# Token numbers of expert tiles: by 0/1 matrix products on TensorE instead of a table of places in DRAM

## Chip, cores, metric

One core of a Trainium2 chip. The time is the device time of one execution in microseconds (us). "Profiled span" is the time from the first to the last instruction in the one execution that was profiled; it is some 2 us shorter than the time of the same execution. Runs are compared with runs of the kernel before on the same chip, fast runs with fast runs; a run is called slow here when it takes over 1.5% more than the fastest one of its kernel.

## The reference, cut

```python
# attention: 8 batches x 8 heads, 576 positions, head size 64, window 32, dilation 4 in half the heads
scores = np.where(masks, scale * q @ k.T, -1e9)
x = softmax(scores) @ v                            # -> (8, 576, 512): 4608 tokens
# experts: 8, each 512 -> 1024 -> 512
for b in range(B):
    prev_e = -1
    for s in range(S):
        fresh_e = int(np.argmax(logits[b, s]))     # logits = x @ w_gate
        if s == 0 or local_gate[b, s] < 0.5:       # local_gate = sigmoid(x @ w_local)
            e = fresh_e
        else:
            e = prev_e if prev_e >= 0 else fresh_e
        prev_e = e
        out[b, s] = p[e] * (np.maximum(x[b, s] @ w1[e], 0.0) @ w2[e])
```

## The kernel before

TensorE first does the attention, two heads at a time (32 "pairs"), and then the experts, in 40 tiles of 128 tokens that have one expert. Every eight pairs complete a "group" of 1152 tokens, which is routed: its tokens' experts are found, and their ranks among the tokens of the same expert. After two groups the first 11 tiles are full and can begin while the attention still runs ("level 0"); the others follow after the fourth group ("level 1"). To begin, a tile needs the list of its tokens, one per partition: token number, gate, and two row numbers in the attention's output.

Before, this list comes from a table in DRAM. Each token is written as a row of four floats (16 bytes) at its place, 128 tokens by one indirect write, nine writes per group; each level then reads its tiles' rows back and transposes them.

```python
def place(g):                                     # (cut) kp = rank of each token within its expert
    nc.vector.tensor_tensor(pl, kp, cst[:TB, C_BASE:C_CODE].unsqueeze(2).to_broadcast(shape), op=Alu.add)
    nc.vector.tensor_tensor(pl, pl, st["oh"], op=Alu.mult)
    nc.vector.tensor_reduce(pf, pl.rearrange("p e j -> p j e"), axis=AX.X, op=Alu.add)
    nc.vector.tensor_copy(pi, pf)
    st["places"] = pi

def scatter(g, j):                                # 9 per group, 36 in all
    i = nc.gpsimd.indirect_dma_start(
        out=tab, out_offset=bass.IndirectOffsetOnAxis(ap=routes[g]["places"][:, j:j + 1], axis=0),
        in_=pay[:, g, j], in_offset=None)

def rows(lv):                                     # one read per level, after all writes so far
    i = nc.gpsimd.indirect_dma_start(out=tr..., in_=tab..., in_offset=...ri...)

def tokens(lv, c):                                # four per level
    tp = bank([P, nt], "tt")
    nc.tensor.transpose(tp, tr[:, :, (2, 3, 0, 1)[c]], ident[:nt, :nt])
    nc.vector.tensor_copy(tiles[what, lv], tp)
```

The order on TensorE is fixed when the program is built. The loop over the pairs counts nominal time ("gaps"); at a gap the next waiting step of the routing is put into TensorE's stream, if its nominal time has passed.

```python
def gap(us):
    gaps[0] += us
    if waiting and gaps[0] - last[0] >= waiting[0][0]:
        last[0] = gaps[0]
        waiting.pop(0)[1]()

def values(n):                                    # (cut) the second product of a pair
    for (a, z), pr in zip(UNITS, prob.pop(n)):
        ...                                       # 20 or 16 products into pv, then VectorE scales
        if not a:
            gap(1.0)                              # a step may stand here, after 20 of the 36

def overlap(n):                                   # the pair's 32 overlapping rows
    nc.vector.tensor_copy(vt[:WIN, :, 1:], vt[QB:, :, :NB - 1])

def idle(times):                                  # products of zeros; also in the kernel before
    to = bank([P, 4, P], "idle")
    for i in range(times):
        nc.tensor.matmul(to, lhsT=blank, rhs=blank.unsqueeze(1).to_broadcast([P, 4, P]), start=True, stop=True, ...)
```

## Time and profile before

| | before |
|---|---|
| median of 3 runs | 788.26 us |
| profiled span | 783.0 us |
| last product on TensorE begins | 770.12 us |
| from there to the end ("tail") | 12.9 us |
| first tile's feature transposes | 160.9 us |
| TensorE clock halved, before the tail | 37.5 us |
| DMAs issued by GpSimd | 241 |

The halved clock is a sum of the trace's clock records (6.8 us from 83.7, 23.9 from 128.1, 6.8 from 281.7). The lines of the slices and of TensorE's timeline are in the prediction.

### The profile page before, as it was taken

How to read it: one execution, taken by the hardware profiler on the slowest of the kernel's cores; microseconds unless marked ns; L12 is line 12 of the kernel's file. 1: busy time of each engine (PE TensorE's matmuls, PEld its weight loads, DVE VectorE, ACT ScalarE, POOL GpSimd, SP SyncE). 2: the span in 40 equal slices, each digit the busy share in tenths (PEclk: the TensorE clock that was granted, in tenths of full speed). 3: DMA queues.
4: the chain of work that ended last, by engine and by line, in shares of the span. 5: the costliest groups of instructions: out<-in, count | busy, mean ns of one | idle time of the engine just before them, and what ended most of it. 6: DMA issues, size and time to landing. Idle time of an engine off the chain costs nothing. (4 is left out here: it accounts for less than half of the span.)

```text
span 783.0 us, 15857 instructions
## 1 busy us (share of the span) xinstructions
PE 745.7 (95%) x6012; PEld 558.9 (71%) x6012; DVE 187.6 (24%) x492; ACT 119.6 (15%) x213; POOL 232.1 (30%) x245
## 2 busy tenths in 40 slices
PE   8999897989999979999999999999999999999993
PEld 5877676977766748678677668677677687687781
DVE  5868494534214110110111010111011011101100
ACT  2545343221120000000001000001001000000000
POOL 1003123232723544312332332332332332333100
PEclk9999897699999989999999999999999999999997
DMA  9868869970584872492167113840113830621000
GB/s 319 302 233 245 232 192 268 410 298 28 120 283 147 183 286 78 149 316 64 35 225 256 35 35 98 306 134 33 34 48 109 306 108 28 194 101 31 25 26 19
DMA packets 37032, 124.06 MB, mean 158 GB/s; under 512 B 7955, under 2 KB 8083, under 8 KB 36944
## 3 DMA queue, kind: packets, MB, share of 16 engines
q1 hardware_dynamic: 27152, 101.92, 39.0%
q0 software_dynamic: 9792, 20.99, 9.7%
q8 instruction: 52, 0.85, 0.5%
q14 instruction: 36, 0.29, 0.1%
HBM read 207.90 MB, written 20.88 MB: 292 GB/s over the span
## 5 line engine op out<-in xcount | busy, mean ns | idle before, releaser
L685 PEld LDWEIGHTS hp<-xe,w1s 128*128 128x128 f32 x2560 | 292.4, 192 | 20.7 <-issue 17.4
L685 PE MATMUL hp<-xe,w1s 128*128 128x128 f32 x2560 | 295.0, 275 | 2.6 <-DVE bad L811 1.5
L700 PE MATMUL yp<-w2s,h 128*128 128x512 f32 x640 | 284.7, 597 | 0.0
L700 PEld LDWEIGHTS yp<-w2s,h 128*128 128x128 f32 x640 | 118.8, 191 | 132.9 <-issue 132.7
L656 POOL DMA_INDIRECT xg<-xd,plain x80 | 76.8, 960 | 263.3 <-PE yp L700 235.5
L689 ACT ACTIVATE h<-hp 128x512 f32<-128x512 f32 x80 | 47.8, 597 | 530.0 <-PE hp L685 530.0
L656 POOL DMA_INDIRECT xg<-xd,dilated x80 | 75.7, 946 | 64.0 <-PE yp L700 55.2
L707 DVE TENSOR_SCALAR y<-yp,gate 128x512 f32<-128x512 f32 x40 | 30.0, 750 | 238.5 <-PE yp L700 130.0
L675 DVE COPY xe<-tp 128x512 f32<-128x512 f32 x40 | 27.6, 691 | 245.1 <-PE tp L673 245.1
L518 POOL DMA_INDIRECT tab<-cst,pi x36 | 35.5, 987 | 115.2 <-DVE x L353 63.5
L294 PE MATMUL sc<-kq 64*96 64x64 f32 x1152 | 62.8, 262 | 6.2 <-DMA kq<-in_qk_dram 5.3
L294 PEld LDWEIGHTS sc<-kq 64*96 64x96 f32 x1152 | 57.3, 175 | 14.7 <-issue 10.3
L708 POOL DMA_INDIRECT out_dram<-y,tok x40 | 40.2, 1006 | 76.5 <-DVE y L707 59.5
L301 DVE SCALAR_TENSOR_TENSOR pr<-sc,mk 96x640 f32<-96x640 f32 x64 | 47.8, 751 | 50.0 <-PE sc L294 33.7
L304 ACT ACTIVATE pr<-pr 96x640 f32<-96x640 f32 x64 | 43.4, 683 | 90.8 <-DVE pr L301 86.9
L347 PE MATMUL pv<-vt,pr 96*64 96x65 f32 x1152 | 45.6, 236 | 4.5 <-issue 4.5
L347 PEld LDWEIGHTS pv<-vt,pr 96*64 96x64 f32 x1152 | 40.2, 148 | 7.3 <-issue 4.8
L370 PE MATMUL tp<-cst,x 128*128 128x128 f32 x144 | 24.5, 309 | 4.0 <-DVE x L353 2.3
L353 DVE TENSOR_TENSOR x<-pv,rec 128x320 f32<-128x320 f32 x64 | 26.8, 449 | 0.1
L673 PE MATMUL tp<-cst,xg 128*128 128x128 f32 x160 | 24.2, 273 | 0.0
L240 DVE COPY vt<-vt 32x1040 f32<-32x1040 f32 x32 | 22.6, 706 | 3.7 <-DMA vt<-in_v_dram 2.8
L370 PEld LDWEIGHTS tp<-cst,x 128*128 128x128 f32 x144 | 17.8, 156 | 7.9 <-PE tp L370 3.2
(109 smaller groups left out, 158.3 us busy)
## 6 DMA issues: line engine op xcount, KB each, us to landing
w1s<-in_w_dram SPq DMA_DIRECT2D x160, 512.0 KB
w2s<-in_w_dram SPq DMA_DIRECT2D x160, 512.0 KB
kq<-in_qk_dram SPq DMA_DIRECT2D x32, 592.0 KB
vt<-in_v_dram SPq DMA_DIRECT2D x32, 292.5 KB
xd<-x SPq DMA_DIRECT2D x16, 576.0 KB
xg<-xd,plain POOLq DMA_INDIRECT x80, 3.0
xg<-xd,dilated POOLq DMA_INDIRECT x80, 3.2
out_dram<-y,tok POOLq DMA_INDIRECT x40, 4.3
```

The source lines that it names most:

```text
L294: here[:] = [nc.tensor.matmul(sc[:KW, u, (i - a) * QB:(i - a + 1) * QB], lhsT=kt[h, i * QB:i * QB + KW], rhs=qt[h, i * QB:(i + 1) * QB], s ...
L301: nc.vector.scalar_tensor_tensor(pr[:, :, :w], sc[:KW, :, :w], -CEIL, mk[:, at:at + w].unsqueeze(1).to_broadcast([KW, 2, w]), Alu.max, Alu ...
L304: nc.scalar.activation(pr[:, :, :w], pr[:, :, :w], Act.Exp, scale=SCALE)
L347: here[:] = [nc.tensor.matmul(pv[u * QB:(u + 1) * QB, i - a], lhsT=pr[:, u, (i - a) * QB:(i - a + 1) * QB], rhs=vt[:, u, i], start=True, s ...
L370: nc.tensor.transpose(tp[:, i].rearrange("p u q -> p (u q)"), x[:, c * w + i].rearrange("p g d -> p (g d)"), ident)
L518: i = nc.gpsimd.indirect_dma_start(out=tab, out_offset=bass.IndirectOffsetOnAxis(ap=routes[g]["places"][:, j:j + 1], axis=0), in_=pay[:, g ...
L656: i = nc.gpsimd.indirect_dma_start(out=xg[t][:, kk], out_offset=None, in_=xd if full == ROWS else xd[:full], in_offset=bass.IndirectOffset ...
L685: here[:] = [nc.tensor.matmul(hp[:, m], lhsT=w1s[t % 2][:, half * FK // 2 + m, kk], rhs=x[:, kk], start=(kk == 0), stop=(kk == DK - 1))]
L689: nc.scalar.activation(ht[t][:, half * FK // 2:(half + 1) * FK // 2], hp, Act.Relu)
L700: here[:] = [nc.tensor.matmul(yp, lhsT=h[:, m], rhs=w2s[t % 2][:, m], start=(m == 0), stop=(m == FK - 1))]
L707: nc.vector.tensor_scalar(y, yp, of_tile("gate", t), None, Alu.mult)
L708: nc.gpsimd.indirect_dma_start(out=out, out_offset=bass.IndirectOffsetOnAxis(ap=of_tile("tok", t), axis=0), in_=y, in_offset=None, bounds_ ...
```

## The change

The intent: no small transfers beside the attention, and no trip through DRAM before the first tile. A token's tile and its place in the tile are known from its rank (`seek`). For each group, `mark` makes two 0/1 matrices on VectorE, "token has place p" and "token is in tile t" (the latter times the four numbers), and `put` multiplies them on TensorE: the sum over tokens is the list.

```diff
-    def scatter(g, j): ...          # 36 indirect writes of places
-    def rows(lv): ...               # 2 reads of the table
-    def tokens(lv, c): ...          # 8 transposes
-    fill ...                        # first contents of the table, 2 DMAs
+    def seek(lv):                   # (cut) tile and place of each token so far
+        q, bound = of_tokens(tiles["off", lv], "q"), of_tokens(tiles["bound", lv], "of_bound")
+        ... q = rank + off, zero where the token is not in this level; hi = q >> 7; at = q - 128 * hi
+    def mark(lv, g):
+        by_place = xp.tile([TB, NJ, P], F32, name="by_place", tag="x")
+        nc.vector.tensor_tensor(by_place, cst[:TB, C_NUM:C_PAY]..., tiles["place"][:, g]..., op=Alu.is_equal)
+        nc.vector.tensor_tensor(there, cst[:TB, C_NUM:C_NUM + nt]..., tiles["tile"][:, g]..., op=Alu.is_equal)
+        by_tile = xp.tile([TB, NJ, TW, nt], F32, name="by_tile", tag="x")
+        for w in range(TW):
+            nc.vector.tensor_tensor(by_tile[:, :, w], there, pay[:, g, :, w]..., op=Alu.mult)
+    def put(lv, g):
+        tp = bank([P, TW, nt], "put")
+        for j in range(NJ):
+            nc.tensor.matmul(tp, lhsT=by_place[:, j], rhs=by_tile[:, j], start=(j == 0), stop=(j == NJ - 1))
+        if not g:
+            tiles["there", lv] = once.tile([P, TW, nt], F32, name=f"there{lv}")
+            nc.vector.tensor_copy(tiles["there", lv], tp)
+        else:
+            nc.vector.tensor_tensor(tiles["there", lv], tiles["there", lv], tp, op=Alu.add)
+        ...
     def route(g):
-        waiting.extend((1.2 if j else 1.5, lambda j=j: scatter(g, j)) for j in range(NJ))
         if lv is not None:
-            waiting.append((0.0, lambda: rows(lv)))
-            waiting.extend((0.0 if c else 12.0 if g == NG - 1 else 9.0, lambda c=c: tokens(lv, c)) for c in range(4))
+            steps.append((1.0, lambda g: seek(lv)))
+            for h in range(g + 1):
+                waiting.append((2.5, lambda h=h: mark(lv, h)))
+                waiting.append((3.5, lambda h=h: put(lv, h)))
```

## The prediction

> **What bounds the kernel now.** I read the page's busy shares first, then the slices, then TensorE's instructions in order of time, then the stretches of 4 us around each hole. The chain that ended last is no help: it holds only the final store.

> ```profile
> PE 745.7 (95%) x6012; PEld 558.9 (71%) x6012; DVE 187.6 (24%) x492; ACT 119.6 (15%) x213; POOL 232.1 (30%) x245
> PE   8999897989999979999999999999999999999993
> DVE  5868494534214110110111010111011011101100
> PEclk9999897699999989999999999999999999999997
> ```

> TensorE is the bound: busy 95% of 783 us, and after about 160 us without a break. VectorE is second, but only in the first 160 us, where the 32 pairs of heads go. The clock line falls in three places (slices 5, 7 to 8, and 15), and a hole in TensorE's stream precedes each. TensorE's timeline has them:

> ```profile
> 80.27 1.75 PE L294 MATMUL sc<-kq 64*96 64x64 f32 x36
> 81.94 0.34 PE L347 MATMUL pv<-vt,pr 96*64 96x65 f32 x4
> 85.70 2.00 PE L347 MATMUL pv<-vt,pr 96*64 96x65 f32 x32 [3.42 <-issue]
> 87.63 2.18 PE L370 MATMUL tp<-cst,x 128*128 128x128 f32 x9
> ...
> 122.32 1.27 PE L347 MATMUL pv<-vt,pr 96*64 96x65 f32 x36
> 128.69 3.15 PE L294 MATMUL sc<-kq 64*96 64x64 f32 x36 [5.10 <-DMA kq<-in_qk_dram]
> ...
> 160.85 0.66 PE L673 MATMUL tp<-cst,xg 128*128 128x128 f32 x4
> ...
> 277.34 1.88 PE L700 MATMUL yp<-w2s,h 128*128 128x512 f32 x4
> 283.21 0.30 PE L610 MATMUL tt<-cst,tr 32*128 32x32 f32 x1 [3.98 <-DMA tr<-tab,ri]
> 283.43 3.78 PE L700 MATMUL yp<-w2s,h 128*128 128x512 f32 x4
> ```

> Holes of 3.42, 5.10 and 3.98 us, and after each the same work takes longer: 36 score products 3.15 instead of 1.75 us, 4 of L700 3.78 instead of 1.88. The first two come while the 9 writes of 128 places each (L518) of a routed group are in the queues; the third is the reading back of the table (L597) itself, at the second level. The first expert tile starts at 160.85, in pair 30. The stretches around the second hole:

> ```profile
> 116.00:120.00 4.00, 3.31 (x68) 2.80 (x66) 3.91 (x11) 1.75 (x3) 3.09 (x4) 1.00 0.63 251
> 120.00:124.00 4.00, 3.42 (x75) 3.05 (x75) 2.75 (x9) 2.30 (x6) 2.90 (x4) 1.00 1.21 219
> 124.00:128.00 4.00, 0.00 (x0) 0.00 (x0) 0.92 (x4) 0.59 (x1) 0.22 (x1) 1.00 0.91 195
> 132.00:136.00 4.00, 4.00 (x45) 3.58 (x43) 1.90 (x6) 1.90 (x4) 0.92 (x1) 0.50 1.01 397
> 136.00:140.00 4.00, 4.00 (x53) 3.81 (x54) 1.51 (x2) 1.24 (x3) 0.00 (x0) 0.50 1.04 421
> ```

> The last three columns are clock, DMA share, GB/s. With the place writes in flight the DMA engines are full (1.21) at 219 GB/s; ten microseconds later they are as full at 397 to 421. The clock stays at 0.50 until about 151.5.

> [...] the L518 writes take 8.5 us (median) to land, 12.1 at most, for 2 KB each. [...] 0.50 from 1.6 us into the hole of 3.42 us and at the end of the one of 5.10, and no drop at waits of 1.07 or 1.46 us. [...] The first hole cuts a run of equal products in two after the fourth, with no semaphore named, so a delayed fetch on full DMA engines is my reading; the trace shows the instruction queue's 52 packets, not the wait. [...]

> **The change, part by part.**

> Removed: 36 writes of places, 2 table reads, the fill of the table, 8 small transposes (0.1 to 0.2 us each), about 8 short VectorE operations per level. GpSimd's time for them (35.5 us) is off every path.
> - Hole 1: 3.42 us, and the slowed work behind it (pv 2.00 for 1.13, turn 2.18 for 1.34, logits 4.60 for 4.22): 2.1. Gain 5.5 us.
> - Hole 2: 5.10 us, and half a clock from 128 to 151.5: 11.7. Gain 16.8 us, provided that nothing else stops TensorE there (see rivals).
> - Hole 3: 3.98 us and 2.8 of slow L700 (3.78 and 2.50 for two times 1.76). Gain 6.8, and 0.6 from the transposes.
> Sum 29.7 us.

> Added on TensorE: a `put` is 9 fp32 products of 128 x 128 stationary by 44 columns (level 0: 4 x 11 tiles) or 128 (level 1: 4 x 32). A program product is two instructions (640 L700 are 40 tiles x 8 products x 2), so 18 each. L685 has the shape of level 1: 64 in 7.31 us, 0.114 each, so 2.06 us per put. I take the same for 44 columns, since loading 128 stationary columns seems to set the pace (4 feature transposes start 0.44 us ahead of what follows, 0.11 each). Level 0 has 2 puts, 4.1 us; level 1 has 4, 8.2 us. All of it is on the bounding engine. Sum 12.3 us.

> Added on VectorE: [...] Level 0: [...] some 6 us, in pairs 21 to 25. A pair lasts 3.68 us there (pairs 4 and 5, 24.27 to 31.63) and costs VectorE 2 x 0.751 + 2 x 0.449 + 2 x 0.166 + 0.706 = 3.44. So it has 0.24 us to spare per pair, and 6 us over five pairs lengthen them by some 5. TensorE's 4.1 us fall into the same pairs, so not both count: I add 2 us to the puts. At level 1 VectorE is a tenth busy and hides its 18 us; but the first put follows seek and mark closely (the emission leaves some 6 us for 6.5), so 1 us of waiting.

> Moved: counting the nominal gaps that the loop hands out, I get the first tile at pair 30 for the kernel before (the trace agrees) and at pair 27 after: the table read's 9 units of wait and the places' 10 go, two marks and puts come. This by itself makes no TensorE work disappear. Its worth is that pairs 28 to 31 lie beside expert work, so the loads of pairs (0.88 MB each) and the first two tiles' weights (8 MB) no longer pace TensorE. As a check by time: pair 18 at 88.8 instead of 94.27, pair 22 at 107.0 instead of 112.47, five pairs with marks and puts 24.8, so pair 27 at 131.8 and the first tile at 133.5; three more pairs remain than before, 11.0 us. 144.5 against 160.85: 16.3 won up to there (5.5 + 16.8 - 6). Level 1 then costs 8.2 + 1.0 - 6.8 - 0.6 = 1.8.

> The two ways agree: 29.7 - 12.3 - 2 - 1 = 14.4, and 16.3 - 1.8 = 14.5. Sum: 788.26 - 14.5 = 773.8; I say **773.5 us**, 1.9% faster.

> **Rivals.**
> - The weights keep the DMA engines full in pairs 21 to 27 with or without places, and TensorE stops there anyway. For it: 1.02 busy from 132 to 168, and 2.2 MB per pair want 5.4 us at 405 GB/s against 3.7 of a pair. Against it: loads go out three pairs ahead, some 11 us, and 1.7 us per pair over six pairs do not use that up; by then the tile has joined. It would give back 5 to 8 us: 779 to 782.
> - VectorE becomes the bound in pairs 22 to 25. The marks take their buffers from the same four as the attention's rows, which are free only when a store to DRAM has landed; [...] VectorE may stop behind it. TensorE would idle long enough to lose its clock again. 778 to 783.
> - The puts cost less: with 44 columns at half the pace, and inside holes that VectorE makes anyway, level 0 is all but free, and short waits of 0.3 to 0.9 us in the pairs vanish under expert work. 767 to 770.
> - Nothing gained: the holes are instruction fetches that come whatever is written. Only hole 3 is then saved and 12 us are added: 790. Against it: a saturated DMA at 397 to 421 GB/s from 132 to 152 stops nothing.

> **Range and chances.** The centre lies almost on the 2% line (772.5). Misses by new waits in pairs 22 to 27 (each a hole plus lost clock, 5 to 9 us) are about as likely as puts and marks that cost 3 to 6 us less than counted. The range is 765 to 783. Faster by over 2%: 0.45; within 2%: 0.52; slower by over 2%: 0.03, as 30 us of holes would all have to stay and the puts cost double.

> **What would show it.** TensorE's busy time 745.7 + 12 less some 8 to 15 us for records made at half clock; clock line at 9 in slices 5 to 8 and 15; no TensorE wait over 2 us between 60 and 160 us and none at level 1; puts as 36 + 72 instructions of 128 x 44 and 128 x 128, 0.11 us apart; first feature transpose near 133 us; marks' comparison 1.2 to 1.4 us; VectorE 9 tenths or more in pairs 22 to 25. I am wrong if a hole over 3 us stands in pairs 22 to 27, if the clock still reads 0.5 there, or if TensorE waits at the puts of level 1.

VectorE's times for `seek` and `mark` (6 us at level 0, 18 at level 1, 6.5 ahead of the first put there) are estimates; no trace of the kernel before has these operations.

## More of the kernel before

One view that I did not read before predicting is the end of the span. These are its stretches of 5 us; the columns are busy time and instructions of PE (TensorE), PEld (its weight loads), DVE (VectorE), ACT (ScalarE) and POOL (GpSimd), then TensorE's clock, DMA share and GB/s:

```profile
770.00:775.00 5.00, 0.71 (x2) 0.00 (x0) 0.75 (x1) 0.00 (x0) 0.97 (x1) 0.82 0.18 61
775.00:780.00 5.00, 0.00 (x0) 0.00 (x0) 0.00 (x0) 0.00 (x0) 0.00 (x0) 0.50 0.02 5
780.00:785.00 5.00, 0.00 (x0) 0.00 (x0) 0.00 (x0) 0.00 (x0) 0.00 (x0) 0.50 0.00 0
```

From about 775 us no engine counts as busy, yet the span ends only at 783.0.

## The result

| | before | after |
|---|---|---|
| median of the 4 runs of this comparison | 788.53 us (787.34 to 790.63) | 793.88 us (793.36 to 795.14) |
| profiled span | 783.0 | 792.3 |
| last product on TensorE begins | 770.12 | 770.64 |
| tail | 12.9 | 21.6 |
| first tile's feature transposes | 160.9 | 148.3 |
| clock halved before the tail | 37.5 | 30.7 |
| DMAs issued by GpSimd | 241 | 201 |

The ratio of fast runs is 1.0067 (95% interval 1.0042 to 1.0092). It divides the mean time of one kernel's fast runs by that of the other's of the same rounds, so it is not quite the ratio of the medians quoted. The change lost 5 us where 14.5 were predicted to be won.

The page of the kernel after, busy shares and two lines of its 40 slices (19.8 us each; a digit is tenths busy, or tenths of the full clock):

```profile
PE 754.4 (95%) x6112; PEld 570.3 (72%) x6112; DVE 205.7 (26%) x535; ACT 119.4 (15%) x213; POOL 194.7 (25%) x205
PE   8999979899999999999999999999999999999990
PEclk9999985899999999999999999999999999999995
```

The clock's falls in slices 5 and 15 are gone, but slices 6 to 8 still show 8, 5, 8. The last PE digit has gone from 3 to 0: TensorE has no work in the last 20 us. TensorE's timeline of the kernel after (start, duration, engine, line, product; in brackets the wait before it; L337 here is L347 before, L284 is L294, L678 is L673):

```profile
111.37 0.80 PE L337 MATMUL pv<-vt,pr 96*64 96x65 f32 x20
116.83 4.07 PE L605 MATMUL put<-by_tile,by_place 128*128 128x44 f32 x18 [4.65 <-DVE by_tile L595]
120.83 1.14 PE L337 MATMUL pv<-vt,pr 96*64 96x65 f32 x16
...
124.00 3.15 PE L284 MATMUL sc<-kq 64*96 64x64 f32 x36
...
140.76 1.75 PE L284 MATMUL sc<-kq 64*96 64x64 f32 x36
...
148.30 0.42 PE L678 MATMUL tp<-cst,xg 128*128 128x128 f32 x2
```

One hole, 4.65 us, before the first `put`, which stands after 20 of the 36 value products of pair 22. From then to about 141 us everything takes almost twice its time: 36 score products 3.15 us instead of 1.75, each `put` 4.07 (2.18 at full clock in e9). VectorE's timeline in the hole shows what TensorE waits for:

```profile
113.63 0.17 DVE L580 TENSOR_SCALAR tile<-tile 128x18 f32<-128x18 f32 x1
113.72 1.35 DVE L587 TENSOR_TENSOR by_place<-cst,at 128x1152 f32<-128x1152 f32 x1
114.99 0.25 DVE L591 TENSOR_TENSOR there<-cst,tile 128x99 f32<-128x99 f32 x1
115.27 0.69 DVE L235 COPY vt<-vt 32x1040 f32<-32x1040 f32 x1
116.00 0.78 DVE L595 TENSOR_TENSOR by_tile<-there,cst 128x99 f32<-128x99 f32 x4
```

The last of `seek` ends at 113.8, and the marks follow with hardly a break, a copy for the next pair (L235) between them. No buffer and no DMA holds VectorE up there: it is simply late. The stretches of 4 us say the same; their columns are as above:

```profile
104.00:108.00 4.00, 3.74 (x74) 3.27 (x75) 3.86 (x23) 1.80 (x4) 0.00 (x0) 1.00 0.72 223
108.00:112.00 4.00, 4.00 (x106) 3.80 (x102) 4.00 (x16) 1.37 (x2) 0.00 (x0) 1.00 0.65 170
112.00:116.00 4.00, 0.17 (x6) 0.03 (x2) 3.94 (x12) 1.30 (x2) 0.00 (x0) 0.69 0.92 351
116.00:120.00 4.00, 3.17 (x15) 3.17 (x16) 2.20 (x8) 0.00 (x0) 0.00 (x0) 0.50 1.01 396
```

From 104 to 116 VectorE (third pair of numbers) is busy 11.80 of 12 us, while TensorE comes down to 0.17 of 4 in the third stretch and the clock with it. And the end of the span of the kernel after:

```profile
770.00:775.00 5.00, 1.23 (x3) 0.19 (x1) 0.75 (x1) 0.00 (x0) 0.97 (x1) 1.00 0.16 57
775.00:780.00 5.00, 0.00 (x0) 0.00 (x0) 0.00 (x0) 0.00 (x0) 0.00 (x0) 0.57 0.03 7
780.00:785.00 5.00, 0.00 (x0) 0.00 (x0) 0.00 (x0) 0.00 (x0) 0.00 (x0) 0.50 0.00 2
785.00:790.00 5.00, 0.00 (x0) 0.00 (x0) 0.00 (x0) 0.00 (x0) 0.00 (x0) 0.50 0.00 0
```

The work ends as before, within half a microsecond; the empty tail is 8.7 us longer. In the tail the trace has instructions that do not count as busy. On GpSimd three long ones stand at the end, two that the trace names INC_SWDGE_SEM and a DRAIN; what comes between and after them is short (0.31 us at most each). Their times from the trace's records, in ns:

```
kernel    GpSimd DMAs   first   second   DRAIN
before    241            732      701     2273
after     201           2082     2070     7832
```

They take 12.0 instead of 3.7 us together, 8.3 us more: nearly the whole difference in the tails.

### The profile page after: what moved, and what is told of

Its sections match the earlier page's. It is cut to its first block, busy times and chain, and to the rows that moved or that the text cites.

```text
span 792.3 us, 15999 instructions
## 1 busy us (share of the span) xinstructions
PE 754.4 (95%) x6112; PEld 570.3 (72%) x6112; DVE 205.7 (26%) x535; ACT 119.4 (15%) x213; POOL 194.7 (25%) x205
## 5 line engine op out<-in xcount | busy, mean ns | idle before, releaser
L284 PEld LDWEIGHTS sc<-kq 64*96 64x96 f32 x1152 | 54.6, 168 | 7.6 <-issue 5.5
L284 PE MATMUL sc<-kq 64*96 64x64 f32 x1152 | 59.8, 256 | 0.2 <-DVE pr L291 0.2
L294 ACT ACTIVATE pr<-pr 96x640 f32<-96x640 f32 x64 | 43.5, 684 | 78.4 <-DVE pr L291 74.2
L337 PE MATMUL pv<-vt,pr 96*64 96x65 f32 x1152 | 44.4, 232 | 0.3 <-issue 0.2
L337 PEld LDWEIGHTS pv<-vt,pr 96*64 96x64 f32 x1152 | 39.0, 144 | 3.5 <-issue 0.6
L360 PE MATMUL tp<-cst,x 128*128 128x128 f32 x144 | 23.5, 299 | 4.2 <-DVE x L343 3.0
L678 PE MATMUL tp<-cst,xg 128*128 128x128 f32 x160 | 24.8, 276 | 1.1 <-DMA xg<-xd,dilated 1.1
L363 ACT COPY xt<-tp 128x384 f32<-128x384 f32 x48 | 21.1, 503 | 25.7 <-PE tp L360 25.1
L235 DVE COPY vt<-vt 32x1040 f32<-32x1040 f32 x32 | 22.3, 697 | 5.2 <-DMA vt<-in_v_dram 4.2
```

The source lines that it names most:

```text
L284: here[:] = [nc.tensor.matmul(sc[:KW, u, (i - a) * QB:(i - a + 1) * QB], lhsT=kt[h, i * QB:i * QB + KW], rhs=qt[h, i * QB:(i + 1) * QB], s ...
L294: nc.scalar.activation(pr[:, :, :w], pr[:, :, :w], Act.Exp, scale=SCALE)
L337: here[:] = [nc.tensor.matmul(pv[u * QB:(u + 1) * QB, i - a], lhsT=pr[:, u, (i - a) * QB:(i - a + 1) * QB], rhs=vt[:, u, i], start=True, s ...
L360: nc.tensor.transpose(tp[:, i].rearrange("p u q -> p (u q)"), x[:, c * w + i].rearrange("p g d -> p (g d)"), ident)
```

## Theories

A: three things ate the gain: (1) the hole before the first `put`, for want of VectorE time; (2) the half clock that follows, because the pairs' small products do not bring the clock back; (3) GpSimd's longer end. B, the rival on the time: the place writes were not what cost time before, the holes come whatever is written. C, the rival on the tail: it belongs to what the last tiles do, not to the number of DMAs.

## The experiments

All results are correct. Every edit is to the kernel after, except where it says otherwise. "Before" is the median of the kernel before on the same chip. "End of work" is the start of the last product; work, tail and half clock are of the profiled run.

| run | median (runs) | before | ratio, 95% | end of work | tail | half clock | first tile | GpSimd DMAs |
|---|---|---|---|---|---|---|---|---|
| e1 | 784.71 | 787.71 | 0.9945 (0.9878 to 1.0011) | 762.86 | 21.2 | 20.5 | 145.0 | 201 |
| e2 | 782.91 | 787.71 | 0.9935 (0.9879 to 0.9991) | 761.75 | 21.2 | 10.2 | 141.6 | 201 |
| e3 | 783.28 | 787.71 | 0.9966 (0.9902 to 1.003) | 764.72 | 13.1 | 13.7 | 142.1 | 237 |
| e4 | 779.53 (3) | 787.71 | 0.9919 (0.9824 to 1.0013) | 764.58 | 13.2 | 13.7 | 141.7 | 237 |
| e5 | 787.89 (1, state unknown) | 786.1 | none | 772.82 | 13.2 | 44.4 | 163.1 | 241 |
| e6 | 794.56 | 786.1 | 1.0112 (1.0041 to 1.0182) | 771.31 | 21.1 | 30.7 | 147.4 | 201 |
| e7 | 786.4 | 786.1 | 1.0 (0.9926 to 1.0075) | 759.82 | 23.8 | 0.0 | 139.6 | 219 |
| e8 | 782.4 (1, state unknown) | 786.1 | none | 767.19 | 13.4 | 13.7 | 147.5 | 237 |
| e9 | 773.02 (6) | 784.28 | 0.9877 (0.9837 to 0.9917) | 758.09 | 13.0 | 0.0 | 137.9 | 237 |
| e10 | 785.11 | 784.28 | 0.9989 (0.9944 to 1.0034) | 768.16 | 21.5 | 30.7 | 143.2 | 201 |
| e11 | 789.12 | 784.28 | 1.0053 (1.0021 to 1.0085) | 766.01 | 21.3 | 10.2 | 144.3 | 201 |
| e12 | 770.17 (5) | 784.28 | 0.9817 (0.979 to 0.9844) | 755.67 | 12.9 | 0.0 | 135.4 | 237 |

The half clock of the table is that of one execution. The mean granted clock of every execution is on record, and within one kernel the time goes with it: e10 took 781.44 and 781.58 us at 0.981 and 0.982, 788.64 and 791.5 (the profiled one) at 0.971; e3 took 779.56 at 0.985 and 787.46 at 0.974. In a span of 780 us, 0.010 of mean clock are some 16 us at half clock (an estimate). So the length of the half clock can change from one execution of a kernel to the next. It is steady in the kernel after (0.969 to 0.973 in eight executions) and in e11 (0.983 or 0.984 in four).

### e5_before_again and e6_after_again: both kernels unchanged, on another chip

> The kernel before, once more, for its trace. If its holes are properties of the program: holes near 82, 123 and 279 us again, of about 3.4, 5.1 and 4.0 us, and half a clock for 7, 24 and 7 us. If they are chance: the hole at 279 (a wait for the table read) again, but the one at 82 (after the fourth row product of a pair, where the run with constant writes back showed 0.67 us and the changed kernel 0.3) shorter than 1.5 us or gone, and the half clock stretches of other lengths, in steps of 3.4 us.

> The changed kernel, once more, on the same chip as the experiments. If the half clock after the hole is a property of the program: 27 us again, last matmul at 771 us, times 793 to 795. If its length is chance: 10 to 27 us, the last matmul between 764 and 771, times 785 to 794. The tail after the last matmul is 21 to 22 us in either case (201 DMAs issued by GpSimd).

The tails (13.2 and 21.1) and the hole before the first `put` (4.67 us) repeat. The half clock of the kernel before varies, 37.5 and 44.4 us, with its holes: the first is 1.90 us here and stands after the same instruction, the second is 4.68. In the kernel after it is 30.7 us both times, and its eight runs lie between 793.4 and 796.5.

### e1_put_late: the level-0 puts later, so that VectorE has time

```diff
-                waiting.append((3.5, lambda h=h: put(lv, h)))
+                waiting.append((3.5 if lv else 7.0, lambda h=h: put(lv, h)))
```

> The changed kernel, with the two puts of level 0 given 7.0 instead of 3.5 nominal units after their marks, so that the first tile joins at pair 29 instead of 27. Theory (the put stands in TensorE's fixed order before VectorE has had time for seek and mark, and the hole costs the clock): no wait of TensorE over 1.5 us between 60 and 160 us, clock 1.00 all through, last work of TensorE 14 to 18 us earlier than in the changed kernel (about 755 instead of 771 us), time 776 to 780. Rival A (VectorE has no time to spare, so the marks lengthen the pairs wherever the puts stand): holes of 2 to 5 us at score or row products, gain under 6 us. Rival B (the weights fill the DMA engines and stop TensorE in pairs 23 to 29): a hole named kq or without a name, half a clock after it.

The hole is gone, but the clock fell all the same. TensorE's timeline of this run:

```profile
114.15 0.55 PE L360 MATMUL tp<-cst,x 128*128 128x128 f32 x3 [1.18 <-ACT xt L363]
...
115.73 3.62 PE L605 MATMUL put<-by_tile,by_place 128*128 128x44 f32 x18
```

The longest wait near it is 1.18 us; the clock is halved for 13.7 us from 116.2 and for another 6.8 from 146.9. The expectation of a full clock missed in this run: in the pairs the clock can fall without a hole worth the name. The gain in work over the kernel after is 7.8 us (762.86 against 770.64), where 14 to 18 were expected. One of the four executions came to the expected time: 778.96 us, at a granted clock of 0.990 against 0.977 in the profiled one.

### e2_fill_hole: ten instructions of zeros in the hole

```diff
         tp = bank([P, TW, nt], "put")
+        if not lv and not g:
+            idle(5)
```

> The changed kernel, with 5 dummy products of 128 x 512 zeros (about 4.4 us) in TensorE's order just ahead of the first put of level 0, where it waits 4.65 us. They take nothing away from the wait. Theory (most of the loss is the clock that stays at half for 27 us after the hole, as pair products are too sparse to bring it back): clock 1.00 from 60 to 150 us, TensorE's last work 11 to 15 us earlier than in the changed kernel. Rival (the clock is a by-product, and the pairs after the hole are paced by loads or VectorE): the clock stays up and the time gains under 4 us.

The `put` comes right behind the zeros and at full clock: it takes 2.18 us instead of 4.07. It starts at 120.52, 3.7 us later than in the kernel after, because there is still one fall of the clock, 10.2 us from 100.3 on, well ahead of the zeros and with no wait over 0.6 us near it; the profiled runs of e7, e9 and e12, which have the same zeros, do not show it. Work ends 8.9 us earlier than in the kernel after; 11 to 15 were expected. The tail stays.

### e3_writes_back: 36 indirect writes back at about their old times, into tables that nobody reads

```diff
+    old_rows = once.tile([TB, NJ], I32, name="old_rows")          # constant row numbers, 256 bytes apart
+    def old_write(g, j):
+        i = nc.gpsimd.indirect_dma_start(
+            out=olds[g], out_offset=bass.IndirectOffsetOnAxis(ap=old_rows[:, j:j + 1], axis=0),
+            in_=pay[:, 0, j], in_offset=None)
     def gap(us):
+        if writes and gaps[0] - wrote[0] >= 1.2:
+            wrote[0] = gaps[0]
+            old_write(*writes.pop(0))
```

> The changed kernel with the 36 writes of 128 rows of 16 bytes put back at about their old times, into tables that nobody reads (index list constant). Theory of the prediction (the writes fill the DMA engines and cause the hole near 82 us): a TensorE hole of 2 to 5 us near 70 to 90 us, 5 to 7 us of time with its clock loss, in that part of the trace. Rival (that hole was chance or belonged to the code's instruction fetch whatever is written): no hole there, and the pairs run as in the changed kernel. Besides: the tail after the last work (20 us in the changed kernel, 11 in the one before): if it depends on the number of GpSimd's DMAs it comes back to about 11 us here as in the run with the writes late; if on something else that the change did, it stays at 20.

The tail falls to 13.1. The writes landed in 4.3 us (median), not in the 8.5 of the kernel before, and where that kernel had its first hole there are only 0.67 us. So this run does not yet test rival B: its writes were too easy. e8 mends that.

### e4_writes_late: the same 36 writes, one in each of the tiles 4 to 39

```diff
     def output(t):
         ...
+        if 4 <= t < 4 + NG * NJ:
+            old_write((t - 4) // NJ, (t - 4) % NJ)
```

> The changed kernel with the same 36 writes, one each in expert tiles 4 to 39, where DMA engines and GpSimd have room. TensorE's last work within 1 us of the changed kernel (771). Theory (the 8.7 us that the changed kernel loses after its last work are GpSimd's end of program, and depend on how many DMAs it has issued): the tail shrinks from 20 to about 11 us and the time to about 785. Rival (the tail comes from something else): the tail stays at 20, time 794.

The tail falls to 13.2 as well, with the writes far from both the pairs and the end: tile 39 is the last. So the tail goes with how many DMAs GpSimd issues (21.2 us with 201 in e1 and e2, 13.1 and 13.2 with 237 in e3 and e4), not with what the writes do nor when; rival C falls. (Each write adds one DMA and 128 rows; which of the two counts, these runs do not separate.) One of the four runs was slow (789.72) and is not used. One point stays open: up to the first `put` this kernel repeats the kernel after, hole included (4.66 us), yet its half clock is 13.7 us and not 30.7, so that its work ends at 764.58 and not at the 771 that was expected; its fast runs spread from 776.3 to 785.6 us, at 0.988 to 0.977 of the clock.

### e7_fill_and_18 and e9_fill_and_36: the zeros, and 18 or 36 late writes

The edits are those of e2 and e4 together; e7 writes only in tiles 4 to 21.

> The changed kernel with the five dummy products ahead of the first put and 18 of the late writes (219 DMAs by GpSimd). From the three counts so far (201, 237, 241: last drain 7.83, 2.12, 2.27 us) I take 39 ns per DMA that is still on the list, all 201 in the first case, 54 and 58 in the others, so that some 183 are taken off the list at a point between 202 and 237. If that point lies before 219: 36 left, last drain 1.4 us, tail after the last matmul about 12 us, time 773 to 780. If it lies after: 219 on the list, drain 8.5 us, tail 22 to 23 us, time 782 to 788. Last matmul at 760 to 763 in either case.

> The changed kernel with the five dummy products ahead of the first put and all 36 late writes (237 DMAs by GpSimd, as in two runs with a last drain of 2.12 us). Last matmul at 760 to 762 us with at most 10 us of half clock, tail 13 us, time 773 to 778: 1.2 to 1.8% faster than the kernel before, and the first version that is clearly faster than both. If the two losses were not independent, the sum would fail: over 782.

The three long instructions at GpSimd's end, from the traces' records (ns):

```
DMAs    run                            first   second   DRAIN
201     after, e1, e2, e6, e10, e11    2082    about 2070   7832
219     e7                             2442    2427     9302
237     e3, e4, e8, e9, e12             692     665     2115
241     before                          732     701     2273
```

They take longer at 219 than at 201 and are short again at 237. So of e7's two cases the second came, but its DRAIN took 9.30 us where 39 ns per DMA gave 8.5: that estimate does not hold, and no record shows the list that it supposes. e7's tail, with 219, was 23.8 us, so e7 is no faster than the kernel before (ratio 1.0) though its work ended 10.8 us before that of the kernel after. e9's profiled run keeps the clock full up to the tail; of its six executions one does not (781.6 us at 0.979, the others 772.31 to 775.79 at 0.992 to 0.995). Its page:

```profile
PE 746.1 (97%) x6122; PEld 560.4 (73%) x6122; DVE 205.9 (27%) x536; ACT 119.0 (15%) x213; POOL 230.8 (30%) x241
PEclk9999999999999999999999999999999999999997
```

and TensorE's timeline, where VectorE is as late as ever (L622 is `put`):

```profile
111.86 4.56 PE L246 MATMUL idle<-blank 128*128 128x512 f32 x10
116.67 2.18 PE L622 MATMUL put<-by_tile,by_place 128*128 128x44 f32 x18 [0.26 <-DVE by_tile L610]
```

The `put` begins at 116.67, against 116.83 in the kernel after: the hole's length is unchanged, it is only filled. Work ends at 758.09 against 770.64: **the half clock was worth some 12.6 us**. e7 agrees: from the last transposes before the hole (106.31 in the kernel after, 106.04 in e9, 107.95 in e7) to the end of work it takes 12.5 us less than the kernel after, e9 12.3.

### e8_true_writes_back: 36 writes at their old times to their true places

```diff
+        nc.vector.scalar_tensor_tensor(pf, st["ef"], float(CAP * P), rank[:, g], Alu.mult, Alu.add)
+        nc.vector.tensor_copy(pi, pf)
     # and the writes of e3, now with
-            in_=pay[:, 0, j]
+            out=tab, out_offset=bass.IndirectOffsetOnAxis(ap=routes[g]["old"][:, j:j + 1], axis=0),
+            in_=pay[:, g, j]
```

> The changed kernel with the 36 writes put back at their old times and with their true, contiguous places (two VectorE operations per group more), into a table that nobody reads. The writes with constant places 256 bytes apart landed in 4.3 us (median) and made a hole of 0.67 us only; in the kernel before they take 8.5 us. If contiguous 16-byte places are what made the writes slow: landing 7 to 10 us, and a hole of 2 to 4 us after the fourth row product near 81 us. If not: landing 4 to 5 us, hole under 1 us, and the hole of the kernel before stays without a cause in the writes. Tail 13 us (237 DMAs).

Here neighbouring ranks of an expert are 16 bytes apart, as in the kernel before. Landing of the 36 writes, e8 and then e3:

```profile
DMA to landing us min/median/max: 2.7/8.3/13.1
```

```profile
DMA to landing us min/median/max: 2.1/4.3/7.1
```

TensorE's timeline at the place of the first hole, e8 and then e3 (L350 and L352 are the value products):

```profile
81.12 0.34 PE L350 MATMUL pv<-vt,pr 96*64 96x65 f32 x4
85.14 1.44 PE L350 MATMUL pv<-vt,pr 96*64 96x65 f32 x32 [3.68 <-issue]
```

```profile
80.89 0.34 PE L352 MATMUL pv<-vt,pr 96*64 96x65 f32 x4
81.89 1.16 PE L352 MATMUL pv<-vt,pr 96*64 96x65 f32 x32 [0.67 <-issue]
```

The hole is back after the fourth product of the same pair: 3.68 us with true places (one execution), 0.67 with easy ones. The kernel after runs these 36 in one piece of 1.61 us, but e4, e9 and e7, whose writes come only in the expert tiles, wait 0.39, 0.39 and 0.94 us at that same product with no place write in flight. So slow place writes stretch something that exists anyway; rival B falls for hole 1. That it is a fetch of instructions fits the fixed place, but no record shows the fetch.

The second hole did not come back. e8 issues the second group's writes from 112.6 to 130.8 us (the kernel before: 112.1 to 123.3), yet its longest wait for kq, the keys and queries of a pair, is 0.67 us, against 5.10 and 4.68 in the two profiles of the kernel before. TensorE stood 4.21 us at the `put` first, which may have given the loads time. So for hole 2 rival B is not refuted: that the writes made it is not shown.

### e10_copies_on_act: the copies of overlapping rows on ScalarE

```diff
-        nc.vector.tensor_copy(vt[:WIN, :, 1:], vt[QB:, :, :NB - 1])
+        nc.scalar.copy(vt[:WIN, :, 1:], vt[QB:, :, :NB - 1])
```

> The changed kernel with the copy of a block's last 32 rows per pair (0.69 us of VectorE) done by ScalarE, which is busy 2.1 of the 3.7 us of a pair. Theory (the hole ahead of the first put is VectorE's lack of time in pairs 21 to 24): the wait at the put shrinks from 4.65 to 0 to 2.5 us, VectorE's share in pairs 20 to 23 from 9.5 to 8 tenths. Rival (the put waits for a chain of dependent operations, whose length does not depend on VectorE's other work): the wait stays over 4 us. Tail 21 to 22 us as in the changed kernel; time 785 to 791 if the hole and with it the half clock goes, 793 if not.

```profile
112.00 4.07 PE L605 MATMUL put<-by_tile,by_place 128*128 128x44 f32 x18 [2.51 <-DVE by_tile L595]
```

Taking some 0.7 us per pair off VectorE cuts the hole from 4.65 to 2.51 us (0 to 2.5 expected; over 4 by the rival). That supports A1. But with 2.51 us the clock was still halved for 23.9 us in the profiled run, and a new wait of 2.38 us for the features of the first tile takes back part of the lead. Work ends only 2.5 us earlier there than in the kernel after. This run is the slowest of the four: two others, at a higher clock (see below the table), took 10 us less.

### e11_burst_after: the hole left as it is, dense products right after it

```diff
             nc.vector.tensor_copy(tiles["there", lv], tp)
+            if not lv:
+                idle(4)
```

> The changed kernel with four dummy products of 128 x 512 just after the first put of level 0, behind the hole, at half clock some 6.8 us. If the clock stays low for 24 to 27 us because the products of the pairs are too sparse to count as busy: back at 1.00 within 3 to 8 us of the burst's start, half clock 7 to 14 us in all, though the burst itself costs most of what that gains (time 789 to 795). If the length is a fixed property of the throttle or chance: 24 to 27 us again and time 797 to 801.

```profile
116.51 4.07 PE L605 MATMUL put<-by_tile,by_place 128*128 128x44 f32 x18 [4.67 <-DVE by_tile L595]
120.37 5.04 PE L246 MATMUL idle<-blank 128*128 128x512 f32 x8
125.34 0.69 PE L337 MATMUL pv<-vt,pr 96*64 96x65 f32 x16
```

The hole is there, the `put` runs at half clock, and 5 us of dense zeros bring the clock back: the 16 value products take 0.69 us against 1.14 in the kernel after. The clock record ends some 2.7 us into the burst. Half clock falls from 30.7 to 10.2 us and work ends 4.6 us earlier, burst included. So dense products end the half clock where the pairs' thin ones did not, A2; the steady clocks of the four executions of e11 and the eight of the kernel after speak against chance. It is no strict rule: in the profiled runs of e3 and e4, which have the same hole and the same pairs behind it, the pairs' products got the clock back after 10.2 us.

### e12_all_three: zeros in the hole, 36 late writes, copies on ScalarE

> The dummy products, the 36 late writes and the copies on ScalarE together. The put has less to wait for, so the dummies (4.4 us) are partly in the way: last matmul within 2 us of the run with the first two alone, time 772 to 779, tail 13 us. If ScalarE's copies delay the exponentials (ScalarE then has 2.9 of 3.7 us per pair): more waits of TensorE in the pairs, 2 to 6 us later.

770.17 us, no half clock, tail 12.9: faster than the kernel before by 1.8% (0.9817, 0.979 to 0.9844) and than every other version here. The last product begins 2.4 us before that of e9 and the time is below the 772 to 779 expected, so the copies on ScalarE gave more than was thought and the waits that were feared did not come. The bound of 2% lies inside the interval, so the verdict at 2% is unclear. The 36 writes do nothing but raise the count of GpSimd's DMAs; that is a trick for this count and this program, not advice.

## Why the prediction was wrong

In profiled spans the prediction of -14.5 us became +9.3, a miss of 23.8. e9 lets the miss be split: without half clock its work ends 12.0 us before that of the kernel before (758.09 against 770.12).

| step | us |
|---|---|
| predicted | -14.5 |
| what remains up to e9's end of work, -12.0 | +2.5 |
| the half clock after it (e9's end of work to that of the kernel after, +0.5) | +12.6 |
| the longer tail | +8.7 |
| measured, profiled spans | +9.3 |

The +2.5 was not measured alone; the hole at the first `put`, 4.65 us where 2 were counted, is about its size, but that this is the whole of it is not shown. The table closes because it is a chain of differences between three profiles. The profiled run of the kernel before was one of its quicker ones; by medians the loss is 5.4 us instead of 9.3.

**The step that failed** is "6 us over five pairs lengthen them by some 5 ... I add 2 us to the puts". It saw rightly that VectorE had 0.24 us to spare per pair, and then treated TensorE as if it gave way evenly. TensorE's order is fixed: it ran the pairs at full speed up to the first `put` (pair 22 began at 106.79, predicted 107.0), and then all of VectorE's backlog fell due in one place. A loss of 5 us in pieces of 1 us and a loss of 4.65 us in one piece are nearly the same sum, but only e1 to e12 show what one piece costs here: the clock, 12.6 us more. The prediction knew this from the holes before (3.42, 5.10 and 3.98 us, with 6.8, 23.9 and 6.8 us of half clock), and named "a hole over 3 us in pairs 22 to 27" as what would prove it wrong.

**What was left out** is the tail. The prediction wrote that GpSimd's 35.5 us for the place writes are "off every path". While the program worked they were (e3 has them back at about their old times, and its work ends no later than in the kernel after), and taking them away still made the program longer, by GpSimd's end (a tail of 21.6 us instead of 12.9). The chain of waits could not show it, since it holds only the last store; span less end of work would have shown that 12.9 us of the end hold almost no work, though not that they would grow.

The rest, step by step:

- Hole 1 (places in the queues): right. It is gone in the kernel after and back in e8; its size varies (3.42 us, 1.90 in e5). In the kernel before the DMA share was 1.17 at 133 GB/s from 82 to 84 us; that a fetch waited behind it is not shown. One reading was off: by the clock record the clock fell 1.4 us into it (83.68, the hole from 82.28), not 1.6. And the slow landing (8.5 us) is not the size's alone: the writes of e3 are as small and landed in 4.3.
- Hole 2 (kq) and hole 3 (table read): both gone. The 16.8 us counted for hole 2 with its clock were however not won, since a new hole stood 11 us earlier and the half clock shrank only from 37.5 to 30.7 us. That the writes caused hole 2 is not shown (e8). The prediction took half the length of a half clock as its cost (11.7 us for 23.5); 30.7 us cost some 12.6 here.
- Level 1: right. Its four `put` of 128 columns take 2.17 to 2.27 us (predicted 2.06), with one wait of 0.49 us (predicted 1).
- Level 0: 2.18 us at full clock (e9), so 44 columns cost as much as 128, as assumed; 4.07 at half clock.
- VectorE's new work, by the trace of the kernel after: the operations of `seek` sum to 2.75 us at level 0 and 3.8 at level 1, those of each `mark` to 2.6 and 3.6, so at level 1 to 18.2 in all. The mark's comparison takes 1.35 us, within the 1.2 to 1.4 given.
- The join: at pair 27, as counted. In time it was 148.3 instead of 133.5. e12 came to 135.4.
- TensorE's busy time: 754.4, above the 743 to 750 expected, as records at half clock are longer.
- Rivals: the second one (VectorE becomes the bound) was nearest, 778 to 783, but through want of time, not through a store that holds a buffer. The first (weights pace TensorE) did not happen: the kernel after has no wait for kq among its waits. "Nothing gained" (790) came nearest to the measured time, for reasons that it did not name.

**Open:** how long the half clock lasts once it has begun. With the same hole it was 30.7 us (after, twice), 13.7 (e3, e4), and without a hole 20.5 (e1), and other executions of e1, e3 and e10 had other clocks. Also open: what made hole 2, why the end of GpSimd costs what it does, and where between 219 and 237 DMAs it falls.

## What to carry to other kernels

When work moves to an engine that is nearly full, do not spread its cost over the phase: find the instruction in the other engine's fixed order that waits for it, and ask how large the backlog is at that place. A hole in a phase of thin products cost several times its length here through the clock (4.65 us and some 12.6 more); dense products of zeros in it kept the clock in e9's profiled run and did not hold up the next product, which still waited 0.26 us for VectorE. And compare span with end of work in both profiles before believing that an engine is off every path.
